# Attention's output product with tokens on partitions: one product of 65 columns, quotients turned back on TensorE

## The chip, the core and the metric

One core of a Trainium2 chip runs the whole program. The metric is device time in microseconds (us). The engines are TensorE (PE in the profile, its weight loads PEld), VectorE (DVE), ScalarE (ACT), GpSimd (POOL) and SyncE (SP, which issues the transfers). Each engine takes its instructions in the order in which the kernel lists them for it.

## The reference

Linear attention, then two multi-layer products. Only the attention is touched:

```python
def phi(x):
    proj = np.einsum('bhsd,df->bhsf', x, w_phi)
    proj = proj - np.max(np.abs(proj), axis=-1, keepdims=True)
    return np.concatenate([np.exp(proj), np.exp(-proj)], axis=-1)
q_p, k_p = (phi(q), phi(k))
kv = np.einsum('bhsf,bhsd->bhfd', k_p, v)
z = np.sum(k_p, axis=2)
num = np.einsum('bhsf,bhfd->bhsd', q_p, kv)
den = np.einsum('bhsf,bhf->bhs', q_p, z)[..., None] + 1e-06
return (num / den).astype(np.float32)
```

There are 4 batches of 8 heads, 576 tokens, a head size of 64, and 128 features, doubled to 256 by the two signs. The attention's result is rearranged to tokens by 512 and passes through `(x@w1)*(x@w2)@w3@w_out`, then `max(x@w_in,0)**2@w_out2`.

## The kernel before, in words

The program has an attention stage of some 190 us, and behind it the two multi-layer products, which are matmuls nearly without a gap. The attention stage also decodes weights for the next stage: entries `w0`, `w1`, `w-1` are steps of one decoded weight (a load, one ScalarE pass, four VectorE operations, a GpSimd addition, then a ScalarE copy and a GpSimd subtraction).

**Pairs and slots.** The attention works on 16 pairs of heads (`live[t]`, four in each batch; `pr` is the pair's number in its batch). One slot of the schedule holds the work of several neighbouring pairs: in slot t the entries with offset 0 work on pair t, those with +1 on pair t+1, those with -1 on pair t-1. The lists `START` (slots 0 to 2), `SLOT` (even slots), `ODD` (odd slots) and `END` (from slot 13) write the order out by hand, and each engine follows it. 512 tokens of a pair are its main part; the remaining 64 (its tail) are worked on two pairs at a time, in extra entries (`project_k2` and `exp_k2` in even slots, `turn_tails` and `keep_tails` in odd ones).

**One slot on TensorE** runs: `project_q` and `project_qt` (projected queries into `pq`), in odd slots `tail_values`, then `project_k0`, `project_k1`, `turn_k` (the next pair's keys), `max_rows` (a transpose of the queries' maxima into `pm`), `out`, `feature_sums`, `turn_q`, in even slots `project_k2`, then `minus_q` (the maxima are subtracted in `pq`), `values0`, `values1` (keys' features times v, into `pkv`).

**What feeds it.** `max_q` and `max_qt` on VectorE read `pq`, `max_rows` turns their result, `max_parts` on VectorE reads `pm`, `send` moves the maxima to one row by a transfer into `mrow`, and `minus_q` waits for it. On ScalarE, `exp_q0`, `exp_q1` and `exp_qt` read `pq` behind `minus_q`, and the next slot's `project_q` may write `pq` only when they are done.

**The output product before.** `out` (`weighted`) multiplies the stationary `kv` (64 columns of values) by the features of 512 tokens, so tokens lie on the free axis, in `po`. `feature_sums` does the same for the tails and, with the stationary `zs` (feature sums repeated over 32 columns), gives the denominators, in `pd`. `keep` and `keep_rest` copy both to `nd` on ScalarE; `denominators` (VectorE), `spread` (eight small GpSimd additions), `reciprocals` (VectorE, with a transpose to `rb`) and `quotients` (GpSimd) give `xm` and `xt`, with model columns on partitions, as the next stage wants them. The PSUM tiles `pm`, `po` and `pd` take turns in two buffers of tag `o`, one bank of 512 columns each.

Of the kernel before, what the change touches and what calls it, by code (L numbers as in the profile page):

```python
# [9 lines left out]
F32 = mybir.dt.float32  # L10
# [7 lines left out]
P = 128  # L18
C = 4
# [12 lines left out]
project_k0/0 low_tail/-1 project_qt/0 max_q/0 max_qt/0 peak_k0/0 fetch_q/0 project_k2/0 keep_rest/0 less_k0/0 exp_k0/0  # L32
max_rows/0 max_parts/0 project_k1/0 send/0 w-1/0 turn_k/0 high_k/0 peak_k1/0 less_k1/0 warm2/0 w0/0 peak_k2/0 exp_k1/0
less_k2/0 store_x/0 w0/0 low_k/0 warm4/0 turn_q/0 minus_q/0 high_q/0 w0/0 values0/0 values1/0 keep_values/0
denominators/0 exp_q0/0 fetch_tails/0 out/0 keep_sums/0 project_k1/1 exp_k2/0 keep/0 fetch_q/1 tail_values/0 spread/0
load_v/0 reciprocals/0 store_x/1 quotients/0 exp_q1/0 exp_qt/0 low_q/0 project_q/1 feature_sums/0 keep_values/1
project_qt/1 project_k0/1 w0/0 fetch_k/1 keep_sums/1 turn_k/1 max_q/1 max_qt/1 w0/1 w-1/1 peak_k0/1 w1/1 max_rows/1
max_parts/1 high_k/1 w1/1 less_k0/1 send/1 low_k/1 peak_k1/1 less_k1/1 exp_k0/1 out/1 turn_q/1 keep/1 exp_k1/1
turn_tails/1 feature_sums/1 high_q/1 denominators/1 spread/1 minus_q/1 exp_q0/1 keep_rest/1 w0/1 values0/1 exp_q1/1
exp_qt/1 low_q/1 w0/1 fetch_q/2 keep_tails/1 w0/1 values1/1 low_tail/1 project_k0/2 w0/2 tail_values/1 fetch_k/2  # L40
project_q/2 reciprocals/1 keep_values/2 project_qt/2 keep_sums/2 quotients/1 max_q/2 max_qt/2 project_k1/2 turn_k/2
max_rows/2 peak_k0/2 less_k0/2 w1/2 high_k/2 max_parts/2 out/2 exp_k0/2 peak_k1/2 fetch_tails/2 send/2 keep/2 load_v/1
less_k1/2 w1/2 feature_sums/2 turn_q/2 w0/2 project_k2/2 low_k/2 denominators/2 peak_k2/2 exp_k1/2 spread/2 less_k2/2
minus_q/2 high_q/2 values0/2 store_x/2 exp_q0/2 exp_q1/2 exp_qt/2 w0/2 w-1/2 w0/2 values1/2 low_q/2 keep_rest/2
reciprocals/2 load_v/2 exp_k2/2 quotients/2
# [14 lines left out]
fetch_k/13 project_q/13 fetch_q/13 project_qt/13 tail_values/12 w0/13 keep_values/13 project_k0/13 max_q/13 max_qt/13  # L60
turn_k/13 w1/13 w1/13 keep_sums/13 max_rows/13 peak_k0/13 less_k0/13 max_parts/13 exp_k0/13 send/13 w-1/13
project_k1/13 store_x/13 out/13 high_k/13 keep/13 feature_sums/13 peak_k1/13 less_k1/13 turn_q/13 low_k/13
turn_tails/13 exp_k1/13 denominators/13 high_q/13 spread/13 minus_q/13 keep_tails/13 x_load/13 keep_rest/13 exp_q0/13
values0/13 w0/13 low_tail/13 exp_q1/13 exp_qt/13 w0/13 values1/13 low_q/13 w0/13 reciprocals/13 quotients/13 load_v/13
tail_values/13 keep_values/14 project_q/14 project_qt/14 keep_sums/14 project_k1/14 max_q/14 max_qt/14 project_k0/14
w1/14 w0/14 peak_k0/14 turn_k/14 less_k0/14 high_k/14 max_rows/14 max_parts/14 send/14 w-1/14 w1/14 exp_k0/14 out/14
feature_sums/14 peak_k1/14 keep/14 less_k1/14 exp_k1/14 low_k/14 turn_q/14 denominators/14 project_k2/14 peak_k2/14
minus_q/14 values0/14 less_k2/14 high_q/14 exp_q0/14 low_q/14 w0/14 w0/14 exp_q1/14 exp_qt/14 values1/14 spread/14
exp_k2/14 keep_rest/14 reciprocals/14 quotients/14 project_q/15 project_qt/15 tail_values/14 late/15 max_q/15
max_qt/15 w0/14 keep_values/15 keep_sums/15 w1/15 w1/15 project_k0/15 peak_k0/15 w0/15 project_k1/15 less_k0/15  # L70
max_rows/15 max_parts/15 peak_k1/15 x_split0/15 feature_sums/15 x_split1/15 exp_k0/15 out/15 send/15 store_x/15
x_split2/15 product_a0/15 keep/15 minus_q/15 denominators/15 spread/15 less_k1/15 w0/15 exp_k1/15 exp_q0/15 w-1/15
values0/15 x_split3/15 values1/15 keep_rest/15 reciprocals/15 turn_w3/15 product_a1/15 w0/15 keep_a/15 split_w3/15
w0/15 tail_values/15 prefetch/15 product_b/16 exp_q1/15 exp_qt/15 keep_values/16 w1/17 keep_sums/16 turn_w3b/16
feature_sums/16 w1/16 early/16 split_w3b/16 w0/17 quotients/15 w0/16 denominators/16 out/16 spread/16 w0/16 gate/16
keep/16 w-1/16 prefetch/17 reciprocals/16 keep_rest/16 last/16 w1/17 w1/16 w0/16 w0/17 w0/17 w0/16 w0/17 quotients/16
prefetch/16
# [4 lines left out]
def attention_then_mlps(ctx: ExitStack, tc: tile.TileContext, q, k, v, w_phi, w1, w2, w3, wo, wi2, wo2, out):  # L82
# [196 lines left out]
    with ExitStack() as actx:  # L279
# [12 lines left out]
        first = {"warm": bank("warm", "o", 2)}  # L292
# [36 lines left out]
        nb = S // 32  # L329
# [208 lines left out]
        def keep_sums(z):  # L538
            z["zs"] = att.tile([P, 2, 2, 32], F32, tag="zs", name=f"zs_{z['nm']}")
            nc.scalar.copy(z["zs"], z["pkv"][:, :, :, D:].to_broadcast([P, 2, 2, 32]))  # L540

        def weighted(z):

            z["po"] = po = bank(f"po_{z['nm']}", "o", 2)
            for e in range(2):
                for j in range(2):
                    nc.tensor.matmul(  # L547
                        po[j * D:(j + 1) * D], z["kv"][:, e, j, :],
                        z["qp"][:, e, j::2, 0:TWO],
                        start=e == 0, stop=e == 1,  # L550
                    )

        def feature_sums(z):

            z["pd"] = pd = bank(f"pd_{z['nm']}", "o", 2)
            for e in range(2):
                for j in range(2):
                    nc.tensor.matmul(
                        pd[j * D:(j + 1) * D, HALF:HALF + TAIL], z["kv"][:, e, j, :],
                        z["qp"][:, e, j::2, TWO:],  # L560
                        start=e == 0, stop=e == 1, skip_group_check=True,
                    )
            for e in range(2):
                for i in range(4):
                    j, s = divmod(i, 2)
                    nc.tensor.matmul(  # L566
                        pd[i * 32:(i + 1) * 32, 0:HALF], z["zs"][:, e, j, :], z["qp"][:, e, 2 * s + j],
                        start=False, stop=e == 1, skip_group_check=True,
                    )

        def keep(z):
            z["nd"] = att.tile([P, S], F32, tag="nd", name=f"nd_{z['nm']}")
            nc.scalar.copy(z["nd"][:, 0:C * P], z["po"])

        def keep_rest(z):
            nc.scalar.copy(z["nd"][:, C * P:], z["pd"][:, HALF:HALF + TAIL])

# [900 lines left out]
```

## Time and profile before

| | |
|---|---|
| median of 3 runs | 909.26 us (907.12 to 909.94) |
| span of the profiled execution, first to last instruction | 904.6 us |
| median less the span | 4.7 us |
| PE busy, of the span | 894.1 us, 99% |
| DVE busy | 660.5 us, 73% |
| ACT busy | 379.4 us, 42% |
| POOL busy | 157.8 us, 17% |

The page gives the span of the profiled execution and no other time of it; what lies around the span is taken as the median's difference. Shares are means over stages with different limits. Ends of pipelined matmuls are modelled, so the chain of waits, which strips the overlap, is the better measure of what a group of matmuls takes.

### The profile page before, as it was taken

What the parts mean: (1) busy time and instruction counts of PE and PEld (TensorE: products, weight loads), DVE (VectorE), ACT (ScalarE), POOL (GpSimd) and SP (SyncE); (2) the same over time, 40 slices, a digit from 0 to 9 for tenths busy, and PEclk for the clock granted to TensorE, in tenths of its full rate; (3) what the DMA queues carried; (4) which work ended last, traced back from release to release, by engine and by line L of the source; (5) the groups of instructions that cost most, each with busy time, mean ns of one, the idle gap of its engine ahead of it and who ended that gap; (6) DMA issues with size and microseconds to landing.
All of it is one profiled execution on the core that took longest, in us unless ns stands there. A gap on an engine that the chain in (4) does not pass through costs nothing.

```text
span 904.6 us, 15198 instructions
## 1 busy us (share of the span) xinstructions
PE 894.1 (99%) x5756; PEld 754.0 (83%) x5756; DVE 660.5 (73%) x1231; ACT 379.4 (42%) x741; POOL 157.8 (17%) x240
## 2 busy tenths in 40 slices
PE   8999999999999999999999999999999999999998
PEld 6667776778888888988888888989899998989896
DVE  7889989979978798789999956466744347643433
ACT  5778887744433434454445422222422123321211
POOL 2566565553222440000000000000000000000000
PEclk9999999999999999999999999999999999999999
DMA  7356564646462436658897899487585754684621
GB/s 216 105 153 159 143 171 141 180 104 164 104 176 73 137 99 222 236 193 268 286 324 282 281 395 334 171 284 245 179 318 195 257 213 170 213 327 162 211 115 70
DMA packets 120648, 182.62 MB, mean 202 GB/s; under 512 B 60736, under 2 KB 80000, under 8 KB 120576
## 3 DMA queue, kind: packets, MB, share of 16 engines
q1 hardware_dynamic: 119520, 180.85, 60.5%
q8 instruction: 45, 0.74, 0.3%
q10 hardware_dynamic: 1056, 0.82, 0.3%
q14 instruction: 27, 0.22, 0.1%
HBM read 140.54 MB, written 40.89 MB: 201 GB/s over the span
## 4 chain that ended last, share of the span: by engine, by line
PE 93%; DVE 3%; DMA 2%; issue 1%; POOL 1%; ACT 0%; SPq 0%; DVEq 0%
PE op L1324 22%; PE pa L258 11%; PE pb L258 11%; PE yp L1037 11%; PE ph_y L1288 8%; PE ph_x L1288 5%; PE ph_w L1288 5%; PE pf L964 5%; PE pkv L518 3%; PE po L547 2%; PE pk L321 2%; PE pq L446 2%; PE pd L566 1%; DMA mrow<-mh 1%; DMA pair<-pair_hbm 1%; PE pq L491 1%
## 5 line engine op out<-in xcount | busy, mean ns | idle before, releaser
L1324 PE MATMUL op<-pair,r 128*128 128x512 f32 x864 | 202.9, 390 | 0.0
L1324 PEld LDWEIGHTS op<-pair,r 128*128 128x128 f32 x864 | 161.8, 188 | 32.2
L1037 PE MATMUL yp<-g,w3o 128*128 128x512 f32 (+1 forms) x480 | 105.3, 368 | 0.0
L1037 PEld LDWEIGHTS yp<-g,w3o 128*128 128x128 f32 x480 | 84.1, 189 | 15.2 <-DVE w3o L224 0.3
L258 PE MATMUL pa<-c,w_w12a 128*128 128x512 f32 (+1 forms) x432 | 93.7, 366 | 0.0
L258 PE MATMUL pb<-c,w_w12b 128*128 128x512 f32 (+1 forms) x432 | 93.6, 366 | 0.0
L1288 PE MATMUL ph_y<-yf_t,pair 128*128 128x384 f32 x432 | 87.2, 335 | 0.0
L258 PEld LDWEIGHTS pa<-c,w_w12a 128*128 128x128 f32 x432 | 75.2, 189 | 13.4 <-DVE c L224 0.3
L258 PEld LDWEIGHTS pb<-c,w_w12b 128*128 128x128 f32 x432 | 75.2, 189 | 13.1
L1288 PEld LDWEIGHTS ph_y<-yf_t,pair 128*128 128x128 f32 x432 | 76.1, 188 | 1.1 <-issue 0.5
L1375 DVE TENSOR_TENSOR u<-ph_y,m 128x384 f32<-128x384 f32 x24 | 13.4, 558 | 71.1 <-PE ph_y L1288 70.0
L1288 PE MATMUL ph_x<-yf_b,pair 128*128 128x384 f32 x288 | 58.5, 337 | 0.6 <-DMA pair<-pair_hbm 0.6
L1204 ACT ACTIVATE g<-g 128x512 fp32r<-128x512 f32 (+1 forms) x39 | 23.0, 590 | 80.8 <-DVE g L1202 80.8
L438 ACT ACTIVATE kp<-kp 128x512 f32<-128x512 f32 (+1 forms) x80 | 47.3, 591 | 15.2 <-DVE kp L431 14.0
L1288 PEld LDWEIGHTS ph_x<-yf_b,pair 128*128 128x128 f32 x288 | 51.2, 188 | 2.9 <-DMA pair<-pair_hbm 1.0
L1301 ACT ACTIVATE r<-m 128x384 fp32r<-128x384 f32 x43 | 22.6, 526 | 73.6 <-DVE m L1300 73.6
L591 POOL TENSOR_SCALAR rc<-dc 32x9 f32<-32x9 f32 x128 | 42.5, 332 | 52.5 <-DVE dc L581 45.4
L964 PE MATMUL pf<-w_wo,w3T 128*128 128x512 f32 x192 | 45.0, 390 | 0.0
L1371 ACT COPY m<-ph_x 128x384 f32<-128x384 f32 x24 | 11.5, 481 | 78.0 <-PE ph_x L1288 78.0
L964 PEld LDWEIGHTS pf<-w_wo,w3T 128*128 128x128 f32 x192 | 36.0, 188 | 8.2 <-issue 0.8
L1302 DVE TENSOR_TENSOR r<-m,r 128x384 fp32r<-128x384 f32 x43 | 24.0, 559 | 25.5 <-ACT r L1301 25.5
L160 DVE SCALAR_TENSOR_TENSOR dt_w<-raw_w,dt_w 128x512 int32<-128x512 int32 x48 | 40.0, 834 | 1.6
(181 smaller groups left out, 1543.9 us busy)
## 6 DMA issues: line engine op xcount, KB each, us to landing
pair<-pair_hbm SPq DMA_DIRECT2D x144, 512.0 KB, 7.6
pair_hbm<-w_w SPq DMA_DIRECT2D x32, 512.0 KB, 6.2
raw_w<-in_moe_w_in_dram SPq DMA_DIRECT2D x16, 512.0 KB, 4.6
raw_w<-in_moe_w_out_dram SPq DMA_DIRECT2D x16, 512.0 KB, 4.4
pair_hbm<-v_w SPq DMA_DIRECT2D x16, 512.0 KB, 6.6
raw_w<-in_moe_w_dram SPq DMA_DIRECT2D x56, 128.0 KB, 3.3
x<-x_hbm SPq DMA_DIRECT2D x12, 512.0 KB, 6.5
yi<-y_hbm SPq DMA_DIRECT2D x12, 384.0 KB, 9.6
```

The costliest lines, as they stand in the source:

```text
L160: nc.vector.scalar_tensor_tensor(out=t, in0=hi, scalar=-(1 << 31), in1=t, op0=ALU.bitwise_and, op1=ALU.bitwise_or)
L258: nc.tensor.matmul(ps[:, 0:n], a, c, start=kk + i == 0, stop=kk == KD - 1 and i == 2)
L438: nc.scalar.activation(z["kp", j][:, :, s, :], z["kp", j][:, :, 1, :], AF.Exp, scale=1.0 - 2.0 * s)
L518: nc.tensor.matmul(z["pkv"][h, s, j], z["kp", j][:, c, s, h], z["vs"][:, j, c, :], start=j + s + c == 0, stop=False, skip_group_check=True,)
L591: nc.gpsimd.tensor_scalar(out=z["rc2"][i * 32:(i + 1) * 32, s, :], in0=z["dc"][at * 32:(at + 1) * 32, :], scalar1=1e-6, scalar2=None, op0= ...
L964: nc.tensor.matmul(pf, a, c, start=n == 0, stop=n == len(todo) - 1)
L1037: nc.tensor.matmul(blk.yp[i][:, 0:blk.n], a, d, start=c == blk.c0 and s == 0, stop=c == blk.c1 - 1 and s == 2)
L1204: nc.scalar.activation(g[:, 0, 0:n], g32[:, 0:n], AF.Copy)
L1288: nc.tensor.matmul(ps_, a, c, start=start and n == 0, stop=n == 5, skip_group_check=not start)
L1301: nc.scalar.activation(r[:, 0], h, AF.Copy)
L1302: nc.vector.tensor_tensor(out=r[:, 1], in0=h, in1=r[:, 0].bitcast(F32), op=ALU.subtract)
L1324: nc.tensor.matmul(z.ops[i], a, d, start=z.p + j + s == 0, stop=z.p == NP2 - 1 and j == 1 and s == 2)
```

## The change

The two operands of the output product change places. The features of 64 tokens (`qp`, half a block of 128) become the stationary operand and `kv` with its 65th column (the feature sum) the moving one, so that `po_t` receives, for 128 tokens on partitions, 64 numerators and the denominator beside them. `po_t` is one PSUM tile of two banks with a single buffer; bank j holds head j of the pair, five spots of 65 columns at most. In pairs with odd `pr` the fifth spot takes the tails of both pairs. `feature_sums`, `denominators`, `spread`, `keep_sums` and `keep_rest` go. `reciprocals` are two small VectorE operations, `quotients` two GpSimd products of tokens by 64. `turn_x`, one slot later, turns the quotients back with four or five 128x128 transposes, into `po_t` too, and `keep_x` copies them to `xm` and `xt` on ScalarE. `max_rows` writes its `pm` into columns 384 to 511 of bank 0 of `po_t`. The last pair is turned in the next stage, in two of that stage's banks. `keep` moves no place in `SLOT` and `ODD`, but copies both banks.

```diff
 SLOT = """
-fetch_q fetch_k project_q project_qt keep_values keep_sums project_k0 max_q max_qt project_k1 w1 w1 w0 turn_k peak_k0
-max_rows high_k less_k0 max_parts send fetch_tails w-1 store_x exp_k0 out feature_sums peak_k1 less_k1 keep turn_q
-low_k project_k2 exp_k1 denominators spread peak_k2 less_k2 high_q minus_q exp_q0 values0 low_q w0 w0 exp_q1 exp_qt
-exp_k2 w0 values1 keep_rest reciprocals quotients load_v
+fetch_q fetch_k project_q project_qt turn_x keep_values keep_x project_k0 max_q max_qt project_k1 w1 w1 w0 turn_k
+peak_k0 max_rows high_k less_k0 max_parts send fetch_tails w-1 store_x exp_k0 out peak_k1 less_k1 keep turn_q low_k
+project_k2 exp_k1 reciprocals quotients peak_k2 less_k2 high_q minus_q exp_q0 values0 low_q w0 w0 exp_q1 exp_qt exp_k2
+w0 values1 load_v
 """.split()
...
-        first = {"warm": bank("warm", "o", 2)}
+        po_t = ps.tile([P, 2, 512], F32, tag="o", bufs=1, name="po")
+        first = {"warm": po_t[:, 0, :]}
...
         def max_rows(z):
 
-            z["pm"] = bank(f"pm_{z['nm']}", "o", 2)[:, 0:P]
+            z["pm"] = po_t[:, 0, 3 * P:4 * P]
             nc.tensor.transpose(z["pm"], z["m1"], ident)
...
-            z["kv"] = att.tile([P, 2, 2, D], F32, tag="kv", name=f"kv_{z['nm']}")
-            nc.scalar.copy(z["kv"], z["pkv"][:, :, :, 0:D])
...
+            z["kv"] = att.tile([P, 2, 2, D + 1], F32, tag="kv", name=f"kv_{z['nm']}")
+            nc.scalar.copy(z["kv"], z["pkv"])
+
+        def spots(z):
+            return 5 if z["pr"] % 2 else 4
 
         def weighted(z):
 
...
+            E = D + 1
+            for j in range(2):
+                for i in range(C):
+                    at = slice((i % 2) * P, (i % 2 + 1) * P)
+                    for e in range(2):
+                        for h in range(2):
+                            half = slice(h * TAIL, (h + 1) * TAIL)
+                            nc.tensor.matmul(
+                                po_t[half, j, i * E:(i + 1) * E], z["qp"][:, e, 2 * (i // 2) + j, at][:, half],
+                                z["kv"][:, e, j, :], start=i + e == 0, stop=e == 1, skip_group_check=True,
+                            )
+                if z["pr"] % 2 == 0:
+                    continue
+                for e in range(2):
+                    for h, y in enumerate((z["before"], z)):
+                        nc.tensor.matmul(
+                            po_t[h * TAIL:(h + 1) * TAIL, j, C * E:(C + 1) * E], y["qpt"][:, e, j, :],
+                            y["kv"][:, e, j, :], start=False, stop=e == 1, skip_group_check=True,
+                        )
 
         def keep(z):
...
+            n = spots(z)
+            z["nd"] = att.tile([P, 2, C + 1, D + 1], F32, tag="nd", name=f"nd_{z['nm']}")
+            nc.scalar.copy(
+                z["nd"][:, :, 0:n], po_t[:, :, 0:n * (D + 1)].rearrange("p j (i d) -> p j i d", d=D + 1)
             )
...
         def reciprocals(z):
...
+            nc.vector.tensor_scalar(
+                out=z["rc"][:, :, 0:n], in0=z["nd"][:, :, 0:n, D], scalar1=1e-6, scalar2=None, op0=ALU.add
             )
+            nc.vector.reciprocal(z["rc"][:, :, 0:n], z["rc"][:, :, 0:n])
 
         def quotients(z):
...
+            for j in range(2):
+                nc.gpsimd.tensor_tensor(
+                    out=z["xd"][:, 0:n, j, :], in0=z["nd"][:, j, 0:n, 0:D],
+                    in1=z["rc"][:, j, 0:n].unsqueeze(2).to_broadcast([P, n, D]), op=ALU.mult,
+                )
+
+        def turned_x(z, at, i):
+            nc.tensor.transpose(at, z["xd"][:, i].rearrange("p j d -> p (j d)"), ident)
+
+        def turn_x(z):
+            for i in range(C):
+                turned_x(z, po_t[:, i // 2, (i % 2) * P:(i % 2 + 1) * P], i)
+            if z["pr"] % 2:
+                turned_x(z, po_t[:, 0, 2 * P:3 * P], C)
+
+        def keep_x_from(z, main, rest):
...
+            nc.scalar.copy(xm[b][:, pr % 2, :].rearrange("p (a n) -> p a n", n=main.shape[-1]), main)
+            if pr % 2:
+                nc.scalar.copy(
+                    xt[:, pr - 1:pr + 1, b * TAIL:(b + 1) * TAIL], rest.rearrange("p (r n) -> p r n", r=2)
                 )
...
-    free = {"u": LEFT - 18, "w": RIGHT}
+    free = {"u": LEFT - 19, "w": RIGHT}
```

`ODD` changes as `SLOT` does (`turn_x` behind `tail_values<`, which there precedes `keep_values`), and so do the written-out slots of `START` and `END`. The exponentials of the queries' tails go to a tile of their own, `qpt`.

## Rows read from the trace of the kernel before

**Rows 1.** The page, part 1: busy us, share of span, instructions.

```profile
PE 894.1 (99%) x5756; PEld 754.0 (83%) x5756; DVE 660.5 (73%) x1231; ACT 379.4 (42%) x741; POOL 157.8 (17%) x240
```

**Rows 2.** An even slot: length; busy us of PE, PEld, DVE, ACT, POOL; clock.

```profile
95.16:105.53 10.37, 10.37 (x134) 7.56 (x134) 9.81 (x20) 7.97 (x17) 6.42 (x13) 1.00 0.49 140
```

**Rows 3.** The chain through two slots: start us, us, what.

```profile
95.16 1.36 PE pq L446 x9
96.52 1.61 PE pk L321 x12
98.13 0.44 PE pkt L360 x4
98.57 0.27 PE pm L469
98.84 1.87 PE po L547 x8
...
102.05 0.58 PE pqt L360 x4
...
103.00 0.51 PE pq L491 x3
103.51 2.02 PE pkv L518 x64
105.53 1.20 PE pq L446 x9
106.73 0.59 PE pkv L528 x8
...
109.49 1.87 PE po L547 x8
...
116.48 1.35 PE pq L446 x9
```

**Rows 4.** The chain from the start of the span.

```profile
19.36 1.18 PE pq L446 x8
...
143.25 3.19 DMA mrow<-mh
```

**Rows 5.** TensorE's timeline, the last `project_q`.

```profile
170.51 0.97 PE L446 MATMUL pq<-qT,wss 64*128 64x512 f32 x6
```

**Rows 6.** ScalarE's timeline: start us, us, instructions, idle before.

```profile
99.79 1.29 ACT L438 ACTIVATE kp<-kp 128x512 f32<-128x512 f32 x2 [0.59 <-DVE kp L431]
100.99 0.57 ACT L573 COPY nd<-po 128x512 f32<-128x512 f32 x1
101.73 1.29 ACT L438 ACTIVATE kp<-kp 128x512 f32<-128x512 f32 x2 [0.17 <-DVE kp L431]
...
103.49 1.94 ACT L498 ACTIVATE qp<-pq 128x1024 f32<-128x1024 f32 x2
...
111.62 0.57 ACT L573 COPY nd<-po 128x512 f32<-128x512 f32 x1
112.37 1.30 ACT L438 ACTIVATE kp<-kp 128x512 f32<-128x512 f32 x2 [0.18 <-DVE kp L431]
...
114.31 1.94 ACT L498 ACTIVATE qp<-pq 128x1024 f32<-128x1024 f32 x2
```

**Rows 7.** VectorE's timeline, from `peak_k0` to `max_parts`.

```profile
98.38 0.65 DVE L421 TENSOR_REDUCE kmax<-pk 128x4 f32<-128x512 f32 x1
99.07 0.69 DVE L431 TENSOR_TENSOR kp<-pk,kmax 128x512 f32<-128x512 f32 x1
99.68 0.27 DVE L474 TENSOR_REDUCE mh<-pm 48x32 fp32r<-48x128 f32 x1
99.88 0.27 DVE L476 TENSOR_REDUCE m<-pm 48x32 f32<-48x128 f32 x1
```

**Rows 8.** Groups by line: count, busy us, mean ns, idle before.

```profile
L610 POOL TENSOR_TENSOR xm<-nd,rb 128x512 f32<-128x512 f32 x16 | 20.9, 1304 | 2.4 <-ACT zs L540 2.3
...
L599 DVE STREAM_TRANSPOSE rb<-rc 128x576 f32<-128x576 f32 x16 | 12.5, 778 | 0.6
```

More of the change, by code (lines that the diff above doesn't have):

```diff
@@ L31 @@
 warm6/0 fetch_k/0 turn_q/-1 turn_k/-1 high_q/-1 low_q/-1 high_k/-1 project_q/0 turn_tails/-1 keep_tails/-1 low_k/-1
[L32 to L45, printed above, removed]
+project_k0/0 low_tail/-1 project_qt/0 max_q/0 max_qt/0 peak_k0/0 fetch_q/0 project_k2/0 less_k0/0 exp_k0/0 max_rows/0
@@ new lines @@
+max_parts/0 project_k1/0 send/0 w-1/0 turn_k/0 high_k/0 peak_k1/0 less_k1/0 warm2/0 w0/0 peak_k2/0 exp_k1/0 less_k2/0
+store_x/0 w0/0 low_k/0 warm4/0 turn_q/0 minus_q/0 high_q/0 w0/0 values0/0 values1/0 keep_values/0 exp_q0/0
+fetch_tails/0 out/0 project_k1/1 exp_k2/0 keep/0 fetch_q/1 tail_values/0 load_v/0 store_x/1 exp_q1/0 exp_qt/0 low_q/0
+project_q/1 keep_values/1 project_qt/1 project_k0/1 w0/0 fetch_k/1 turn_k/1 max_q/1 max_qt/1 w0/1 w-1/1 peak_k0/1 w1/1
+max_rows/1 max_parts/1 high_k/1 w1/1 less_k0/1 send/1 low_k/1 peak_k1/1 less_k1/1 exp_k0/1 out/1 turn_q/1 keep/1
@@ new lines @@
+exp_k1/1 turn_tails/1 high_q/1 reciprocals/1 quotients/1 minus_q/1 exp_q0/1 w0/1 values0/1 exp_q1/1 exp_qt/1 low_q/1
+w0/1 fetch_q/2 keep_tails/1 w0/1 values1/1 low_tail/1 project_k0/2 w0/2 tail_values/1 fetch_k/2 project_q/2
+keep_values/2 project_qt/2 turn_x/2 keep_x/2 max_q/2 max_qt/2 project_k1/2 turn_k/2 max_rows/2 peak_k0/2 less_k0/2
+w1/2 high_k/2 max_parts/2 out/2 exp_k0/2 peak_k1/2 fetch_tails/2 send/2 keep/2 load_v/1 less_k1/2 w1/2 turn_q/2 w0/2
+project_k2/2 low_k/2 reciprocals/2 quotients/2 peak_k2/2 exp_k1/2 less_k2/2 minus_q/2 high_q/2 values0/2 store_x/2
@@ L46 @@
+exp_q0/2 exp_q1/2 exp_qt/2 w0/2 w-1/2 w0/2 values1/2 low_q/2 load_v/2 exp_k2/2
 """.split()
 SLOT = """
[L48 to L51 removed]
+fetch_q fetch_k project_q project_qt turn_x keep_values keep_x project_k0 max_q max_qt project_k1 w1 w1 w0 turn_k
@@ L56 @@
-low_k turn_tails exp_k1 denominators spread high_q minus_q keep_tails exp_q0 values0 low_q w0 w0 exp_q1 exp_qt w0
-values1 keep_rest low_tail reciprocals quotients load_v tail_values
+fetch_q fetch_k project_q project_qt tail_values< turn_x keep_values keep_x project_k0 max_q max_qt project_k1 w1 w1
+w0 turn_k peak_k0 max_rows high_k less_k0 max_parts send w-1 store_x exp_k0 out peak_k1 less_k1 keep turn_q low_k
+turn_tails exp_k1 reciprocals quotients high_q minus_q keep_tails exp_q0 values0 low_q w0 w0 exp_q1 exp_qt w0 values1
@@ L58 @@
+low_tail load_v tail_values
 """.split()
 END = """
[L60 to L77, printed above, removed]
+fetch_k/13 project_q/13 fetch_q/13 project_qt/13 tail_values/12 turn_x/13 w0/13 keep_values/13 keep_x/13 project_k0/13
+max_q/13 max_qt/13 turn_k/13 w1/13 w1/13 max_rows/13 peak_k0/13 less_k0/13 max_parts/13 exp_k0/13 send/13 w-1/13
@@ new lines @@
+project_k1/13 store_x/13 out/13 high_k/13 keep/13 peak_k1/13 less_k1/13 turn_q/13 low_k/13 turn_tails/13 exp_k1/13
+reciprocals/13 quotients/13 high_q/13 minus_q/13 keep_tails/13 x_load/13 exp_q0/13 values0/13 w0/13 low_tail/13
+exp_q1/13 exp_qt/13 w0/13 values1/13 low_q/13 w0/13 load_v/13 tail_values/13 keep_values/14 project_q/14 project_qt/14
+turn_x/14 keep_x/14 project_k1/14 max_q/14 max_qt/14 project_k0/14 w1/14 w0/14 peak_k0/14 turn_k/14 less_k0/14
+high_k/14 max_rows/14 max_parts/14 send/14 w-1/14 w1/14 exp_k0/14 out/14 peak_k1/14 keep/14 less_k1/14 exp_k1/14
@@ new lines @@
+reciprocals/14 quotients/14 low_k/14 turn_q/14 project_k2/14 peak_k2/14 minus_q/14 values0/14 less_k2/14 high_q/14
+exp_q0/14 low_q/14 w0/14 w0/14 exp_q1/14 exp_qt/14 values1/14 exp_k2/14 project_q/15 project_qt/15 tail_values/14
+turn_x/15 late/15 max_q/15 max_qt/15 w0/14 keep_values/15 keep_x/15 w1/15 w1/15 project_k0/15 peak_k0/15 w0/15
+project_k1/15 less_k0/15 max_rows/15 max_parts/15 peak_k1/15 x_split0/15 x_split1/15 exp_k0/15 out/15 send/15
+store_x/15 x_split2/15 product_a0/15 keep/15 minus_q/15 reciprocals/15 quotients/15 less_k1/15 w0/15 exp_k1/15
@@ L78 @@
+exp_q0/15 w-1/15 values0/15 x_split3/15 values1/15 turn_w3/15 product_a1/15 w0/15 keep_a/15 split_w3/15 w0/15
+tail_values/15 prefetch/15 product_b/16 exp_q1/15 exp_qt/15 keep_values/16 w1/17 turn_w3b/16 turn_x/16 keep_x/16 w1/16
+early/16 split_w3b/16 w0/17 w0/16 out/16 w0/16 gate/16 keep/16 w-1/16 prefetch/17 reciprocals/16 quotients/16 last/16
+w1/17 w1/16 w0/16 w0/17 w0/17 w0/16 w0/17 prefetch/16
 """.split()
@@ L553, in feature_sums @@
[L553 to L569, printed above, removed]
@@ L571, in keep @@
-        def keep(z):
[L572 to L576, printed above, removed]
-        def denominators(z):
-            z["dc"] = att.tile([P, nb // 2], F32, tag="dc", name=f"dc_{z['nm']}")
-            nc.vector.tensor_reduce(
-                z["dc"], z["pd"][:, 0:HALF].rearrange("p (n r) -> p n r", r=32), AX.X, ALU.max, apply_transpose=True
-            )
@@ L713, in attention_then_mlps @@
             "turn_tails": (1, even(turn_tails)), "keep_tails": (1, even(keep_tails)), "low_tail": (1, even(low_tail)),
-            "out": (-1, weighted), "keep": (-1, keep), "keep_rest": (-1, keep_rest),
+            "out": (-1, weighted), "keep": (-1, keep), "turn_x": (-2, turn_x), "keep_x": (-2, keep_x),
             "tail_values": (0, tail_values), "reciprocals": (-1, reciprocals),
-            "feature_sums": (-1, feature_sums), "denominators": (-1, denominators), "spread": (-1, spread),
             "quotients": (-1, quotients), "store_x": (-2, store_x),
```

61 lines of the change are left out of this document (21 added, 40 removed).

## The prediction, made before the changed kernel ran

> **What bounds the kernel now.** I read the page first: PE is busy for 99% of the span [rows 1], so the question is what the attention stage costs TensorE, and whether anything else stands close behind it. Next the busy times slot by slot: in the slot of pair 8, 10.37 us long, TensorE has no gap, but VectorE works 9.81 us and ScalarE 7.97 us of it, and the granted clock is 1.00 [rows 2]. Then the chain of waits over two slots: it stays on TensorE from one `project_q` to the next, 95.16 to 105.53 (even slot, 10.37) and 105.53 to 116.48 (odd slot, 10.95), 10.66 on average [rows 3].
>
> The busy share of ScalarE hides what its order does. In its timeline `exp_k0` ends at 101.08, `keep` starts at 100.99, `exp_k1` at 101.73, and after `high_q` `exp_q0` and `exp_q1` run from 103.49 to 105.43 [rows 6]. The next `project_q` overwrites what they read, and it starts at 105.53 [rows 3]. So in an even slot a second chain, ScalarE's from `keep` to `exp_q1`, ends 0.1 us before TensorE is through. In the odd slot it ends at 114.31 + 1.94 = 116.25, and `project_q` starts at 116.48: 0.23 us. The reader is to see here a kernel with two bounds that nearly touch, where the second begins with a copy of the very product that changes.
>
> **The change on TensorE.** Removed: `out`, 1.87, and `feature_sums`, from 100.71 (98.84 + 1.87) to 102.05, 1.34; together 3.21 us a slot [rows 3]. Added: 32 products of 65 columns against 64 stationary columns for a pair with even `pr`, 40 with odd `pr`. No row shows the new product, but `values0` and `values1` have its shape: 32 products of 65 columns by 64 in 64 instructions, in alternating halves, 2.02 us [rows 3]. By columns alone, from the 1.87 us of `out` (8 instructions of 512 against 64 of 65), it would be 1.90. I take 2.02, the same form, and for 40 products 2.53. If the halves didn't overlap it would be twice that, but the row of the same form says that they do. `turn_x` is four or five transposes; `turn_k` does four in 0.44 [rows 3], so 0.44 and 0.55.
>
> In an even slot `out` works on an odd pair: 10.37 - 3.21 + 2.53 + 0.44 = 10.13. In an odd slot: 10.95 - 3.21 + 2.02 + 0.55 = 10.31. On average 10.22, 0.44 less than before. If TensorE stayed the bound, this would be the gain.
>
> **The change elsewhere.** VectorE loses the transpose to `rb`, 0.78 [rows 8], and two shorter operations, and gets two operations on ten elements a partition; it stays below its 9.81 of [rows 2], so I cost this at nothing. GpSimd loses eight small additions, and its product of 512 columns (1.30) becomes two of 256 or 320, between 1.30 and 1.65 us together [rows 8]; the quotients are wanted only by `turn_x` of the next slot, some 5 us after `keep`, so they are covered. On ScalarE `keep` copies 520 or 650 elements in place of 512 at 0.57; between that row and an exponential of 1024 elements (1.94 for two) I take 0.58 and 0.70 [rows 6]. `keep_x` (0.57, and 0.2 more in odd slots) stands behind `keep_values`, about 2 us before `high_k` can start, where ScalarE waits now; if that cover were gone, it would delay `exp_k0`, which has over 1 us before `keep`. `keep_sums` and `keep_rest` go from the same place.
>
> **What the order does with it.** Now the second chain, step by step from the start P of `project_q`. `turn_x` pushes `project_k0` back: in an even slot it ends at P + 1.36 + 0.44 + 0.81 (half of 1.61) = 2.61; in an odd one at 1.20 + 0.59 + 0.55 + 0.81 = 3.15 [rows 3]. Then VectorE does `peak_k0`, `less_k0` and the two reads of `pm` in `max_parts`: 98.38 to 99.88 + 0.27, 1.77 us [rows 7]. Before, `out` went into the other buffer of tag `o`, and ran while VectorE was at this. Now `pm` lies in bank 0 of `po_t`, and the first new product writes other columns of that bank. I take it that the program lets it wait until `max_parts` has read `pm`, since the tile is one buffer; no row of before shows such a wait, and the case without it is a rival below. With 0.1 us for each hand-over (the 105.43 to 105.53 above), `out` starts at P + 4.58 (even) and 5.12 (odd), where TensorE could have started at 4.12 and 4.51 (1.36 + 0.44 + 1.61 + 0.44 + 0.27; 109.49 - 105.53 + 0.55).
>
> The Trainium skill (PSUM — Partial Sum Buffer, section "PSUM bank collisions raise a hardware error") says that accesses of two engines must be kept apart by bank and quadrant of partitions, and not by address. By that rule the wait is due and the sum is the forecast's; by addresses alone it would be that of the second rival. No run here shows yet which holds.
>
> `out` ends at 4.58 + 2.53 = 7.11 and 5.12 + 2.02 = 7.14. `keep` needs the whole product. From `keep` to the end of `exp_q1` it takes 105.43 - 100.99 = 4.44 now, less 0.17 of waiting, plus 0.13 for the longer copy: 4.40; in an odd slot 116.25 - 111.62 = 4.63, less 0.18: 4.45 [rows 6]. With two hand-overs the next `project_q` starts at P + 7.11 + 0.1 + 4.40 + 0.1 = 11.71 (even) and 7.14 + 0.1 + 4.45 + 0.1 = 11.79 (odd). So the slot is 11.75 us in place of 10.66, and TensorE, with 10.22 us of work, waits twice in it: before `out`, and before `project_q`.
>
> `minus_q` doesn't add to that: its row arrived up to 3.19 us after `max_parts` where it was waited for [rows 4], that is by 4.58 + 3.19 = 7.8 or 8.3, and `exp_q0` can't start before 9.6 in any case.
>
> **The sum.** From the `project_q` of pair 1 (19.36) to that of pair 15 (170.51) are 14 slots in 151.15 us [rows 4, 5]. After: 14 x 11.75 = 164.5, 13.35 more. Behind that no `project_q` follows and TensorE has products of the next stage to run: three sets of transposes (1.54) and two new products (2.02 + 2.53) replace 6.42 us, 0.33 less; the wait before `out` of pair 14 remains (0.6). In all +13.6. The next stage is a TensorE stage without slack, so this carries through: 904.6 + 13.6 = 918.2 of span, and with the 4.7 us between span and median 922.9 us.
>
> **Rivals.** *TensorE's sum decides (faster).* If ScalarE's chain came through in time, 14 slots of 10.22 are 143.1, 8.05 less, and with the 0.33 the time is 900.9. For it: PE is the chain everywhere in [rows 3], and VectorE is relieved. Against it: the chain may grow by 0.1 us in an even slot before it decides, and `out` ends 1.1 us later in it (P + 6.65 even without any wait, against 5.55).
>
> *The wait for `max_parts` isn't there.* Then `out` starts at 4.12 and 4.51, and the slot is 4.12 + 2.53 + 0.2 + 4.40 = 11.25 or 4.51 + 2.02 + 0.2 + 4.45 = 11.18. 14 x 11.2 = 157.0, +5.9, less 0.33: 914.8 us. Still slower, by the late `keep` alone.
>
> *Hand-overs cost more.* `keep` starts 0.28 us after the end of `out` now (100.71 to 100.99) [rows 3, 6]; ScalarE was at `exp_k0` until about then, so how much of it is hand-over can't be seen. If each of the two or three on the chain takes that, a slot grows by up to 0.4 more, 5.5 in all: 928.
>
> *Nothing measurable:* the removed VectorE work gives back what the copy costs. VectorE set the slots' length only in few slots (the 14 average 10.80 against 10.66), some 2 us; that doesn't cover 5.9.
>
> **How the numbers follow.** The forecast has 0.70, the missing wait 0.14, dearer hand-overs 0.06, the faster case 0.07, no change 0.03. About 0.3% (2.7 us) can be told from no change. Faster is thus 0.07, same 0.03, slower 0.90. The forecast's own range, with the hand-over between 0.05 and 0.2 and the product between 1.90 and 2.1, is 918 to 927; the range of 8 in 10 reaches to 913, to take in part of the case without the wait, and to 928.
>
> **What would show it.** The groups by line should show `out` with 64 or 80 instructions, near 2.0 and 2.5 us in the chain, and a wait of TensorE before it that ends with `max_parts`, some 0.5 us a slot. TensorE should sit idle before `project_q` until `exp_q1` ends, some 1 us a slot, and the chain of the attention stage should pass through ScalarE's `keep`, `exp_k1` and `exp_q`. The start of the last `project_q` should be 13 us later. VectorE's busy time in a slot should fall by about 1 us. I am wrong if the slots come out near 10.2, or if TensorE's waits end at something that this sum doesn't have: the quotients before `turn_x`, or `keep_x` before `max_rows`.

## The result, and the profile after

The changed kernel takes 918.63 us (median of 4 runs, 918.14 to 918.78) against 908.34 us for the kernel before in the same comparison (4 runs, 907.12 to 909.94): a ratio of 1.0118, with a 95% interval of 1.0105 to 1.013. It is 1.2% slower. The profiled execution has a span of 916.8 us at a granted clock of 0.999; before it was 904.6, so the span grew by 12.2 us. Executions of one kernel differ with the granted clock (the two-tile kernel below took 906.3 to 907.8 us at 0.999 and 1.000, and 909.8 to 911.8 at 0.996 to 0.998), so small differences are read by the ratios' intervals.

The page of the changed kernel, part 1, answers to [rows 1].

```profile
PE 886.7 (97%) x6468; PEld 775.1 (85%) x6468; DVE 646.0 (70%) x1215; ACT 382.4 (42%) x733; POOL 112.5 (12%) x112
```

TensorE's busy time fell by 7.4 us although the span grew: the change did take work from the engine that was the bound, and the engine now waits. The same in windows, an odd slot and the even one behind it (start:end, length; busy us of PE, PEld, DVE, ACT, POOL; clock), to be held against [rows 2]:

```profile
87.06:98.76 11.70, 10.37 (x184) 9.22 (x184) 8.68 (x18) 9.38 (x21) 3.73 (x4) 1.00 0.74 214
98.76:110.42 11.66, 10.29 (x184) 9.09 (x185) 9.20 (x20) 8.22 (x17) 3.94 (x4) 1.00 0.39 109
```

Both slots are 1.3 to 1.4 us longer than TensorE's work in them. The chain of waits of the changed kernel through the even slot shows where that goes (start us, us, what), where the chain of [rows 3] stays on TensorE:

```profile
99.65 0.35 DVE tT L360
...
100.04 0.32 PE pq L440
100.36 0.59 PE po L586 x4
100.95 0.73 PE pk L316 x6
...
101.70 0.70 DVE kmax L415
...
103.03 0.27 DVE mh L468
103.31 0.21 DVE m L470
...
103.56 1.15 PE po L545 x32
104.71 0.23 PE po L553 x8
104.95 0.93 PE po L545 x32
105.88 0.26 PE po L553 x8
...
106.16 0.70 ACT nd L561
106.86 0.54 ACT kp L432
...
107.42 0.63 ACT kp L432
108.06 0.48 ACT qT L357
108.54 1.84 ACT qp L492 x2
...
110.42 1.25 PE pq L440 x9
```

It comes from VectorE, where `low_tail` (99.65) holds the last part of `project_qt` back until 100.04. From there it leaves TensorE twice: behind `project_k0` (L316) to VectorE (`peak_k0`, L415, then `less_k0` and `max_parts`, L468 and L470) and back at the new product (L545, L553), then to ScalarE at `keep` (L561) and back at the next `project_q` (L440), with `exp_k1`, `high_q` and the two `exp_q` between. TensorE's timeline of the changed kernel has the same two gaps as idle time, in brackets with what ended it:

```profile
92.20 2.09 PE L545 MATMUL po<-kv,qp 128*64 128x65 f32 x64 [0.64 <-DVE m L470]
...
98.76 0.97 PE L440 MATMUL pq<-qT,wss 64*128 64x512 f32 x6 [0.69 <-ACT qp L492]
...
103.56 1.15 PE L545 MATMUL po<-kv,qp 128*64 128x65 f32 x32 [0.64 <-DVE m L470]
...
110.42 0.97 PE L440 MATMUL pq<-qT,wss 64*128 64x512 f32 x6 [0.29 <-ACT qp L492]
```

Over the attention stage, 25 to 185 us, the groups of waits give the two their sums (us in total, times, longest):

```profile
PE po L545 <- DVE m L470: 9.5, 13, 1.3
...
PE pq L440 <- ACT qp L492: 6.1, 10, 0.8
```

### The profile page after: what moved, and what is told of

It is laid out like the page before. It is cut to its first block, busy times and chain, and to the rows that moved or that the text cites. A ratio compares the mean times of both kernels' runs of the same rounds, so it can differ in the third digit from the quotient of the medians.

```text
span 916.8 us, 16526 instructions
## 1 busy us (share of the span) xinstructions
PE 886.7 (97%) x6468; PEld 775.1 (85%) x6468; DVE 646.0 (70%) x1215; ACT 382.4 (42%) x733; POOL 112.5 (12%) x112
## 4 chain that ended last, share of the span: by engine, by line
PE 86%; ACT 4%; DVE 4%; DMA 4%; issue 2%; SPq 0%; DVEq 0%
PE op L1321 21%; PE pa L252 11%; PE pb L252 10%; PE yp L1028 10%; PE ph_y L1285 8%; PE ph_x L1285 5%; PE ph_w L1285 5%; PE pf L955 5%; PE po L545 3%; DMA pair<-pair_hbm 2%; PE pq L440 2%; ACT kp L432 1%; PE pk L316 1%; DVE kmax L415 1%; ACT qp L492 1%
## 5 line engine op out<-in xcount | busy, mean ns | idle before, releaser
L252 PEld LDWEIGHTS pb<-c,w_w12b 128*128 128x128 f32 x432 | 75.2, 189 | 13.1
L432 ACT ACTIVATE kp<-kp 128x512 f32<-128x512 f32 (+1 forms) x80 | 47.2, 590 | 8.1 <-DVE kp L425 6.8
L545 PE MATMUL po<-kv,qp 128*64 128x65 f32 x1024 | 34.7, 223 | 11.9 <-DVE m L470 11.2
L545 PEld LDWEIGHTS po<-kv,qp 128*64 128x64 f32 x1024 | 31.8, 138 | 15.6 <-DVE m L470 14.7
```

The lines of the kernel that those rows point to most:

```text
L252: nc.tensor.matmul(ps[:, 0:n], a, c, start=kk + i == 0, stop=kk == KD - 1 and i == 2)
L432: nc.scalar.activation(z["kp", j][:, :, s, :], z["kp", j][:, :, 1, :], AF.Exp, scale=1.0 - 2.0 * s)
L545: nc.tensor.matmul(po_t[half, j, i * E:(i + 1) * E], z["qp"][:, e, 2 * (i // 2) + j, at][:, half], z["kv"][:, e, j, :], start=i + e == 0, ...
```

## The experiments

Each was timed beside the kernel before on the same chip, whose median was between 906.6 and 907.7. "Changed" is the kernel after the change. The runs ask three things: whether the late `keep` is on the chain at all, whether the order alone does it, and what the wait at the shared tile costs.

**ScalarE's chain: the copy done twice.** From the changed kernel.

```diff
-            nc.scalar.copy(z["nd"][:, :, 0:n], ...)
+            for _ in range(2):
+                nc.scalar.copy(z["nd"][:, :, 0:n], ...)
```

> The changed kernel with keep's copy done twice. Theory (keep lies on the chain that sets the slot's length): each of the 14 slots grows by the second copy, 0.5 to 0.6 us, in all 7 to 8 us: 926 us. Rival (ScalarE has time to spare, as its busy share says): no change, 918.6.

Measured: 929.72 us, ratio 1.0248 (1.0217 to 1.028), against 926 expected. The profiled execution, the shortest of the four, has a span of 925.8, 9.0 more than the changed kernel. That is 14 times 0.64: a copy of 0.59 or 0.70 us is paid nearly in full in every slot, so `keep` is on the chain. The wait it lengthens is the one before `project_q`; the one before the product stays as it was:

```profile
PE pq L440 <- ACT qp L492: 13.8, 12, 1.4
...
PE po L545 <- DVE m L470: 9.5, 13, 1.4
```

**The order alone.** The kernel before, with its old product and its old denominators; only the two stages on TensorE change places, in the two repeated orders and in the written-out ones, so that `out` ends later and `keep` with it.

```diff
-... exp_k0 out feature_sums peak_k1 less_k1 keep ...
+... exp_k0 feature_sums out peak_k1 less_k1 keep ...
```

> The kernel before, with feature_sums ahead of out on TensorE in slots 1 to 14: the same work, the same engines, but the product that keep copies ends 1.34 us later. Theory (ScalarE's chain from keep to exp_q1 stood 0.1 to 0.2 us behind TensorE and becomes the bound): even slots 11.5 and odd ones 11.9 us in place of 10.37 and 10.95, in all 11 to 14 us more, 919 to 922 us. Rival (the slowdown came from the new product itself, or from the shared tile): no change, 908.

Measured: 916.96 us, ratio 1.011 (1.0093 to 1.0126), 9.3 more than before and 2 less than the 919 to 922 expected. TensorE has the same instructions as before, and yet a loss nearly as large as the changed kernel's is there. It is not the same sum: the changed kernel has less work on TensorE, and a wait that this one lacks. Its chain of waits:

```profile
93.26 1.89 PE po L547 x8
...
95.18 0.59 ACT nd L573
95.76 0.54 ACT kp L438
...
104.93 1.91 PE po L547 x8
...
106.87 0.59 ACT nd L573
...
109.14 1.84 ACT qp L498 x2
...
111.02 1.03 PE pq L446 x6
```

The reader is to see `keep` (here L573) and the exponentials on it, as in the changed kernel, with no product of 65 columns in sight. So the second bound that the prediction read in [rows 6] was real: 1.3 us of delay of `out` are enough to make it the first.

**`keep` behind `exp_k1`.** From the changed kernel: the copy moves one place down ScalarE's queue (in `SLOT` as shown, and likewise in `ODD` and in the written-out slots, as in the runs below), so that `exp_k1` needn't wait for the product.

```diff
-... less_k1 keep turn_q low_k project_k2 exp_k1 reciprocals ...
+... less_k1 turn_q low_k project_k2 exp_k1 keep reciprocals ...
```

> The changed kernel with keep moved behind exp_k1 in ScalarE's order, in slot 1 and in slots 3 to 14; no work differs. Theory (ScalarE's chain from keep to exp_q1 sets the slot): exp_k1 no longer waits for the product, the chain is peak_k1, less_k1, exp_k1, keep, high_q, exp_q, and the slot falls from 11.7 to about 10.9 us; 13 slots give some 10 us, so 908 us. Rival (only the wait before the product counts, ScalarE's order does not): no change, 918.6. Rival (TensorE's own work has grown): no change.

Measured: 916.5 us, ratio 1.0096 (1.0081 to 1.0111): 2.1 us less than the changed kernel, not 10. The two slots looked at go from 11.66 and 11.70 to 11.48 (98.63 to 110.11) and 11.09 (to 121.20), because other chains stand right behind the one that was moved. Of the slots written out by hand some got longer: the first two take 23.0 us in place of 21.5, the last 12.8 in place of 12.0, which eats a part of the gain. The chain of waits of this kernel goes in the even slot through the transfer of the query maxima to `minus_q` (L485), in the odd one through VectorE to `exp_k1` (L432):

```profile
104.17 3.08 DMA mrow<-mh
...
107.39 0.75 PE pq L485 x3
...
116.06 0.70 DVE kp L425
...
116.78 0.64 ACT kp L432
```

Both start behind the late `max_parts`, which this move doesn't touch. A third follows from the move itself: `reciprocals` on VectorE waits for `keep`, and the weight steps and `low_tail`, on which `project_qt` waits, stand behind it in VectorE's order. VectorE's wait there is 13.1 us over the stage in the changed kernel, and here:

```profile
DVE rc L568 <- ACT nd L561: 19.0, 14, 2.0
```

**`max_parts` earlier.** From the changed kernel: the rows of maxima are turned and read ahead of `peak_k0`, so that the shared tile is free when TensorE reaches the product.

```diff
-... project_k0 max_q max_qt project_k1 w1 w1 w0 turn_k peak_k0 max_rows high_k less_k0 max_parts send ...
+... project_k0 max_q max_qt max_rows max_parts project_k1 w1 w1 w0 turn_k peak_k0 high_k less_k0 send ...
```

> The changed kernel with max_rows moved ahead of project_k1 and max_parts ahead of peak_k0, in slots 1 to 14, so that the maxima have been read from po_t before TensorE comes to the product; no work differs. Theory (the product waits for the reading of the maxima, and what is late there passes on to the next project_q): the product starts 0.45 to 0.6 us earlier, 14 slots give some 7 us, 911.5 us. Rival (the wait is covered, since ScalarE's chain alone sets the slot's length): no change, 918.6.

Measured: 921.63 us, ratio 1.0155 (1.0136 to 1.0174): slower than the changed kernel. The gap before the product is gone, but VectorE comes late with `less_k0`, for a reason that no theory had. Its timeline and GpSimd's:

```profile
104.44 0.28 DVE L468 TENSOR_REDUCE mh<-po 48x32 fp32r<-48x128 f32 x1 [0.66 <-PE po L463]
104.65 0.27 DVE L470 TENSOR_REDUCE m<-po 48x32 f32<-48x128 f32 x1
104.96 0.99 DVE L471 TENSOR_TENSOR mh<-m,mh 48x32 fp32r<-48x32 f32 x1
```

```profile
104.63 1.27 POOL L179 TENSOR_TENSOR w_wo<-dt_wo,w_wo 128x512 fp32r<-128x512 f32 x1 [1.19 <-ACT w_wo L177]
```

The subtraction of 32 elements a partition (L471), 0.18 us in the changed kernel, ends at 105.95, when GpSimd's subtraction over 512 elements ends (105.90), and `peak_k0` and `less_k0` stand behind it.

**The same without GpSimd's subtraction.** From the previous one: where a step of the weight preparation subtracts on GpSimd, it writes zeros.

```diff
-        nc.gpsimd.tensor_tensor(out=dst[:, 1], in0=w[0], in1=dst[:, 0].bitcast(F32), op=ALU.subtract)
+        nc.gpsimd.memset(dst[:, 1].bitcast(F32), 0.0)
```

> As the run with the maxima read early, but GpSimd's subtraction in the weights' decoding is a memset: the low parts of six decoded weight blocks of the first product and of the eight of w_out are left out (zero). Theory (in that run the last small VectorE operation of max_parts took 0.99 us in place of 0.18 because it was held until GpSimd's subtraction had ended, and that ate the gain): the operation takes 0.18 us again, the slots fall by about 0.7 us, and the time is 910 to 913 us. Rival (the operation is slow because of what it reads or where it stands, not because of GpSimd): 0.99 us stays, 921.6.

Measured: 914.12 us, ratio 1.0079 (1.0064 to 1.0095), 7.5 less, and 1 us above the 910 to 913 expected. The line's instructions, with the subtraction on GpSimd (first) and without it (second); durations are min/median/max in ns:

```profile
L471 DVE TENSOR_TENSOR mh<-m,mh x16: 182/992/997, 11.3 to 189.3; 48x32 fp32r<-48x32 f32 x16
```

```profile
L471 DVE TENSOR_TENSOR mh<-m,mh x16: 182/184/186, 11.6 to 181.7; 48x32 fp32r<-48x32 f32 x16
```

So the overlap is the cause of the 0.99 us. The Trainium skill (SBUF — State Buffer, section "Who interferes with whom") says that a VectorE instruction with two inputs in SBUF contends with a GpSimd instruction that reads SBUF, and not with one that only writes it. The first half agrees with the 0.99 us. The second half no run here shows, because in no slot do the zeros run beside L471; in the even one they are written 1 us before it starts:

```profile
99.66 0.53 POOL L179 MEMSET w_wo<- 128x512 f32 x1
```

```profile
101.23 0.18 DVE L471 TENSOR_TENSOR mh<-m,mh 48x32 fp32r<-48x32 f32 x1
```

Without the subtraction this order is 0.39% faster than the changed kernel: a second way, with the tile left as it is, by which the missing wait gives time back. It isn't the whole of what the wait costs, since reading the maxima first keeps `peak_k0` waiting: in the odd slot the chain runs from `max_parts` through `peak_k0`, `less_k0` and `exp_k0` to `keep`.

**Both moves together.** `keep` behind `exp_k1` and `max_parts` ahead of `peak_k0`, from the changed kernel.

> Both moves together: keep behind exp_k1, and the maxima read early. Theory: the product is off the chain that sets the slot, which now runs over max_q, max_parts, peak and less on VectorE, exp_k1, keep, high_q, exp_q: 10.5 us in even slots and 11.1 in odd ones, about as with keep moved alone, 906 to 909 us. If the two waits were independent costs they would add: 901. Rival (TensorE's own work has grown): no change, 918.6.

Measured: 931.13 us, ratio 1.0253 (1.0236 to 1.0271), 22 us or more above what was expected. GpSimd's subtraction holds VectorE as in the run before last (L471 takes 0.99 us in the median), and ScalarE waits 13.9 us in the stage for `less_k0` and `less_k1`, 1.5 in the changed kernel. But with `max_parts` moved alone that wait is 17.0 us, so it doesn't explain the 9.5 us that this run is slower than that one. Two things are new against it: VectorE waits 16.6 us at `reciprocals` for the late `keep`, in place of 0.9, and the granted clock over the stage (25 to 185 us) is 0.97, with stretches of 10 us at 0.83, in place of 1.00. How the 9.5 us divide between them, no run separates. Two moves that each take a wait away were worse together than either.

**Two tiles in place of one.** From the changed kernel: a bank of its own for each head's product, the head whose bank doesn't hold the maxima's rows first, and a copy for each bank, in `keep` and in `keep_x`. The work on TensorE is the same; no stage is moved.

```diff
-        po_t = ps.tile([P, 2, 512], F32, tag="o", bufs=1, name="po")
+        po_t = [ps.tile([P, 512], F32, tag=f"o{j}", bufs=1, name=f"po{j}") for j in range(2)]
...
-            for j in range(2):
+            for j in (1, 0):
                 for i in range(C):
...
-            nc.scalar.copy(z["nd"][:, :, 0:n], ...)
+            for j in (1, 0):
+                nc.scalar.copy(z["nd"][:, j, 0:n], ...)
```

> The changed kernel with a tile of its own for each of the two banks, head 1 (the bank without the maxima) multiplied first, and keep and keep_x as one copy for each bank. Theory (the product waits until the maxima have been read, because they share the tile): head 1 starts right behind max_rows and covers the reading, the gap before the product goes, and the second copy alone lies behind it. Odd slots should fall from 11.7 to about 10.9 us; in even ones the maxima's transfer comes next, as in the run with keep moved, at 11.4; in all some 7 us less, 911 us. Rival (the gap has another cause): the gap stays and the time is 918.6 or more, from the added copies.

Measured: 907.62 us (10 runs), ratio 1.0015 (0.9999 to 1.0032): no difference from before that can be told, some 9 us less than the changed kernel, and 3 less than the 911 expected. TensorE's timeline in the even slot:

```profile
97.52 0.27 PE L463 MATMUL po<-ident,m 128*128 128x128 f32 x1
97.72 1.15 PE L545 MATMUL po<-kv,qp 128*64 128x65 f32 x32
...
101.97 0.76 PE L485 MATMUL pq<-mrow,minus 128*128 128x512 f32 x3 [0.75 <-DMA mrow<-mh]
...
104.70 0.97 PE L440 MATMUL pq<-qT,wss 64*128 64x512 f32 x6
```

The product follows the maxima's transposes (L463) with no gap. What waits now is `minus_q`, for the transfer of the maxima; the slot is 11.05 us, still more than TensorE's 10.3. Over the 14 slots the mean is 10.84, against 10.80 before.

**Which half of that it was.** The two-tile kernel takes the wait away and also hides one of two copies behind the second head's products. Two more kernels separate these; each differs from it by one order.

```diff
 first:   the head with the maxima's bank is multiplied first
-            for j in (1, 0):
+            for j in (0, 1):
                 for i in range(C):
...
-            for j in (1, 0):
+            for j in (0, 1):
                 nc.scalar.copy(...)
 second:  the products as in the two-tile kernel, the copies the other way round
-            for j in (1, 0):
+            for j in (0, 1):
                 nc.scalar.copy(...)
```

> Two tiles of a bank each, but the head whose bank holds the maxima's rows is multiplied first, so the product waits for max_parts as in the changed kernel, while the copy of that first bank can run behind the second head's products. If the wait is what costs, only the copy's hidden half is gained: 0.70 to 0.41 and 0.59 to 0.38 on the chain, 0.25 a slot, 14 slots, 3.5 us: 915. If instead the hidden copy is what gave the 11 us of the two-tile kernel, 908 to 910, with the wait of about 0.64 us before the product still in TensorE's timeline.

> Two tiles, the bank without the maxima's rows multiplied first, so the wait is gone, but the copies go in the order that both stand behind the end of the whole product. If the wait is what costs, the product starts 0.65 us earlier a slot, some 9 us in 14 slots, less about 0.1 us a slot for a second copy: 910 to 912. If the hidden copy is what counts, about 916 to 918, with no wait before the product.

Measured: with the wait, 915.12 us, ratio 1.0093 (1.008 to 1.0106); without it and with both copies behind the product, 911.63 us, ratio 1.0051 (1.0036 to 1.0066). Both came out as the wait's theory had them. TensorE's timeline with the wait (first), and TensorE's and ScalarE's without it (second and third):

```profile
102.40 1.15 PE L545 MATMUL po<-kv,qp 128*64 128x65 f32 x32 [0.64 <-DVE m L470]
```

```profile
96.61 0.97 PE L440 MATMUL pq<-qT,wss 64*128 64x512 f32 x6 [0.32 <-ACT qp L492]
...
100.69 1.15 PE L545 MATMUL po<-kv,qp 128*64 128x65 f32 x32
...
107.62 0.97 PE L440 MATMUL pq<-qT,wss 64*128 64x512 f32 x6
...
112.05 2.09 PE L545 MATMUL po<-kv,qp 128*64 128x65 f32 x64
```

```profile
103.29 0.77 ACT L562 COPY nd<-po 128x325 f32<-128x325 f32 x2 [0.82 <-PE po L553]
```

By the ratios, from 1.0118 for the changed kernel: the hidden copy alone gives back 0.25%, the missing wait alone 0.67%, both 1.03%. That is about 2.3, 6.1 and 9.4 us, each to within some 2 us, and the sum of the two agrees with the third. The larger part is the wait. What these runs don't separate is the tile from the order: the changed kernel's first products go to the very bank that holds `pm`, and with that bank first the wait is there with two tiles as well. One tile with the other bank multiplied first was not run, so whether the wait goes by the tile or by the bank stays open. It does not go by columns alone.

**Three attempts to go below the kernel before,** all from the two-tile kernel: `keep` behind `exp_k1`; the two copies on VectorE (`nc.vector.tensor_copy` for `nc.scalar.copy`); `max_rows` ahead of `turn_k` and `max_parts` between `peak_k0` and `less_k0`.

> The two tiles, and keep behind exp_k1 as well. Theory: the product is off the chain; what stays is VectorE's way from project_k0 to less_k1 and the maxima's transfer, which the two tiles do not move: 11.4 us in even slots, 11.0 in odd ones, 909 to 913 us, little better than the two tiles alone. If the gap and ScalarE's order were independent costs they would add: 907 or less.

> The two tiles, and keep on VectorE in place of ScalarE, at the same place of the order. Theory: ScalarE's chain loses keep (0.55 us), VectorE gains 0.7 to 0.8 us behind less_k1, where it waits now; the slot is again that of the maxima's transfer and of exp_k1: 909 to 912 us. Rival (VectorE becomes the bound, through low_k and low_q): 915 or more.

> The two tiles, and max_rows ahead of turn_k, max_parts between peak_k0 and less_k0, in slots 1 to 14. Theory (with two tiles the slot is set by the maxima's way: max_parts, the transfer, minus_q, exp_q): that way starts 0.4 to 0.6 us earlier, less_k0 comes 0.7 us later where ScalarE has some slack; even slots fall by 0.4 us, odd ones by 0.1, 14 slots give 3 to 4 us, 904 us, below both kernels. Rival (TensorE's or ScalarE's sum sets the slot with two tiles): no change, 907.6.

Measured: 913.88 (ratio 1.0076, 1.0053 to 1.01), 911.15 (1.0047, 1.0025 to 1.0069) and 912.94 us (1.0065, 1.005 to 1.008). The second is in its range, the first 0.9 us above it, the third a plain miss; all three are slower than the two-tile kernel. In the third's timeline of VectorE, L471 again takes some 0.7 us in odd slots, beside a subtraction on GpSimd, and `exp_k0` is late by it. In all three, ScalarE's wait for `less_k0` and `less_k1` stands among the longest of the stage (7.5, 14.1 and 9.9 us in total, 2.8 in the two-tile kernel). Only in the third was something put in ahead of `less_k0`. In the first two ScalarE comes to `exp_k1` without having waited for the product and copied it, and so waits for `less_k1`. The first has besides VectorE's wait at `reciprocals` for the late `keep`, 19.7 us in place of 2.2. No version beat the kernel before.

## Why the prediction held

**Two bounds that nearly touch.** Right. The swapped order of the kernel before, with TensorE's work untouched, costs 9.3 us, and a second `keep` in the changed kernel lengthens the wait before `project_q`.

**TensorE's sum.** 10.13 and 10.31 us were worked out for the two kinds of slot; 10.29 and 10.37 were busy. The product took 2.58 us (even; from 103.56 to 106.14) and 2.11 (odd) for 2.53 and 2.02, and `turn_x` 0.59 (even) and 0.70 (odd) for 0.44 and 0.55: together more than the difference. The rival by which this sum decides fails in the changed kernel, and even without the wait and with the copy half hidden the mean slot was 10.84, not 10.22.

**The wait for the shared tile.** Right, and it is the larger of the two parts. The new product writes columns 0 to 324 of the bank, `pm` lies in columns 384 to 511, and yet it starts 0.04 us behind `max_parts`; where the first products go to a tile that doesn't hold `pm`, it starts behind L463 without a gap. The start was predicted at P + 4.58 and 5.12 and came at 4.80 and 5.14. The 0.22 in the even slot comes with a wait that the sum didn't have: `project_qt` waited for `low_tail` on VectorE (the row at 99.65), where a step of the weight preparation stands ahead of it, so that `turn_x` starts at P + 1.60 in place of 1.36. Longer transposes and shorter hand-overs cancel about. That the cause is one buffer for two banks was the prediction's reason; the runs show a wait for `pm`'s bank or tile and not which. Whether the chip itself would mind a product beside a read in one bank, which the rule that the prediction takes from the Trainium skill (PSUM — Partial Sum Buffer) is about, no run shows either: in no run does the product run into the bank that is being read.

**The rival without the wait** had the product at P + 4.12 and 4.51. In the kernel with the wait gone and both copies behind the product it starts at 4.08 (100.69 - 96.61) and 4.43, and the time is 4.6 us above before (0.51%) where the rival had 5.5. So the rival was sized well; it was not what the changed kernel did.

**ScalarE's chain.** From `keep` to the end of `exp_q1` 4.40 and 4.45 were predicted. It took 4.22 (106.16 to the end of the row at 108.54, 110.38) and 4.38 (94.33 to 98.71 in ScalarE's timeline). The hand-overs, taken as 0.1 each, are 0.02 to 0.04 in the chain. These two small errors and the late `project_qt` nearly cancel, which is luck: slots of 11.66 and 11.70 against 11.71 and 11.79. "Dearer hand-overs" is thereby out.

**The sum.** The `project_q` of pair 1 starts at 18.88 and that of pair 15 at 181.07: 14 slots in 162.2 us, 11.0 more than the 151.15 of [rows 4, 5], where 13.35 was predicted.

```profile
18.88 0.96 PE L440 MATMUL pq<-qT,wss 64*128 64x512 f32 x6
...
181.07 0.97 PE L440 MATMUL pq<-qT,wss 64*128 64x512 f32 x6
```

The last 12 of them take 140.7 (from 40.34), and 12 x 11.75 is 141.0. Nearly the whole error is in the first two, whose order is written out for itself: 21.5 in place of 23.5. From the last `project_q` to the next stage's first product after the attention it is 27.3 us (to 208.40) against 26.6 (170.51 to 197.12), +0.7 for +0.27. Of the 12.2 us that the span grew, the remaining 0.9 (12.2 - 11.0 - 0.7, and 0.5 by which pair 1 starts earlier) lie behind 208.40, in the later stages, and were not followed.

**From span to time.** 4.3 us separate the forecast of 922.9 from 918.63. 2.9 of them are the 4.7 us that were put between span and median: in the changed kernel they are 1.8 (918.63 - 916.8). In every other run, too, the time of the profiled execution is 1.8 us more than its span, so the profiled execution of the kernel before took some 906.4 us by estimate (904.6 + 1.8), less than any of its timed runs. Its distance to their median is scatter between executions, not something that a change carries along.

**What would show it.** 64 instructions in the odd slot and 80 in the even one, the wait before them that ends with `max_parts`, the idle time before `project_q` that ends with `exp_q1`, and the chain through `keep`, `exp_k1` and `exp_q` are all there. Some sizes differ. The idle time before `project_q` is 0.29 to 0.69 us a slot and not 1. The last `project_q` is 10.6 us later and not 13, and VectorE's 9.81 us became 9.20 in the even slot, 0.6 less and not 1. The quotients and `keep_x`, named as what could prove it wrong, are not on the chain. Two waits that the sum didn't have do stand in it, both small: that of `project_qt` above, and 2.2 us over the stage in which `minus_q` waits for the maxima's row. In the even slot `minus_q` starts at P + 8.60 (107.36 in TensorE's timeline), where its row was reckoned to be there by 7.8; `exp_q0` comes at P + 9.78, so it adds nothing there, as was said.

## What to carry to other kernels

When the busiest engine has no gap, look for the chain that ends just ahead of it: here ScalarE's ended 0.1 to 0.2 us before TensorE needed it, so saving 0.3 us of TensorE's work a slot while its product ended 1.4 to 1.8 us later lost time. A product can wait for another engine's read of other columns, if both lie in one tile and bank: here 0.64 us a slot. A tile for each bank, the free bank multiplied first and a copy for each bank took back nearly all that the change had lost. Before an operation is moved, look at what else waits for its result: `keep` behind `exp_k1` freed ScalarE, and held up `reciprocals` and with it VectorE. Moves within an order that is tight on several engines don't add up, and two that were meant to help separately were slower together than either alone.

## What was not expected of the hardware

- VectorE's subtraction of 32 elements a partition with both inputs in SBUF takes 182 ns alone and up to 997 ns beside GpSimd's subtraction of 512 elements (1.27 us), ending within 0.05 us of it where both are shown; without that subtraction beside it, it takes 184.
- The transfer of the query maxima, issued by SyncE, lands 1.8 us behind its issue in the median and 3.8 us at most in the changed kernel. Why some are twice as slow stays open. In the two-tile kernel `minus_q` waits 6.4 us for it over the stage; that it sets that kernel's time is not shown, and moving it ahead lost time.
- A wait through a semaphore between engines shows as 0.02 to 0.04 us in the chain.
